# Slot outputs in two PSUM banks, a direct product for the first columns of S, a first gh in pieces, and dispatch maxima read from PSUM

## The chip, the core and the metric

The kernel runs on one NeuronCore of a Trainium2 chip. The metric is the device time of one execution in microseconds (us), median of several runs. A profile is one execution recorded by the hardware profiler; its span is a little shorter than that execution's device time. The engines are named PE (TensorE matmul), PEld (TensorE weight load), DVE (VectorE), ACT (ScalarE), POOL (GpSimd) and SP (SyncE, which issues the DMAs).

## The reference

Three stages follow each other; all data is fp32.

```python
# 1. attention: 8 batches, 8 heads, 576 queries of 64; keys and values are means over groups of 8
k_p = k.reshape(B, H, 72, 8, D).mean(axis=3);  v_p = the same of v
x = softmax(q @ k_p.T / 8) @ v_p               # x: 4608 tokens x 512
# 2. soft mixture of 8 experts with 4 slots each (32 slots)
logits = x @ phi
d = exp(logits - logits.max(0)); d /= d.sum(0)  # dispatch: over tokens
slot_input = d.T @ x                            # 32 x 512
slot_out[e] = relu(slot_input[e] @ w1[e]) @ w2[e]   # 512 -> 1024 -> 512
c = exp(logits - logits.max(1)); c /= c.sum(1)  # combine: over slots
x = c @ slot_out
# 3. feed-forward, 512 -> 2048 -> 512
g = s * relu(x @ w_in) ** 2 + b
out = g @ w_out
```

## The kernel before, in words

**Attention and dispatch.** A loop runs over 36 token tiles of 128 in a software pipeline of stages A to F; an order written out by hand (`LOOP`, `FIRST`, `PLAN1`, `PLAN2`) says in which order an iteration issues them, and each engine executes what it is given strictly in that order. Stage A transposes q (L362 on PE, copied by ACT at L364), B makes the scores (PE L392), their row maxima (DVE L399) and the difference (DVE L401), C the exponential (ACT L409), its sum (DVE L410) and the product P (POOL L430), D transposes P (PE L443, ACT L449), E and F make logits. `p` advances the pooling of k and v for the next pair of batches (DVE and POOL, L260 to L265; ACT L282). `r` advances every running `dispatch` by one piece, up to its next `yield`. A `dispatch` (one for each batch, eight in all) finds the 32 maxima of its batch's logits: a matmul at L558 spreads them over all partitions into a PSUM bank, DVE copies them to `m_all` (L559), one `r` later DVE subtracts them from the logits into `dd` (L562), one `r` later ACT takes the exponential (L564), and later ones sum `dd` (L569) and multiply it with P (PE L586). Matmul outputs of this stage take turns in a pool of four PSUM banks (`bank()`).

**Experts.** 32 weight tiles of 1 MB are loaded and used in the order of `EORD`; matmuls of the first layer are at L969, those of the second at L977. At L977 four matmuls with 32 output rows each (four quarters of the partitions) take 512 columns, in the bank `so_ps`, summed over all experts. An fp32 matmul shows as two records in the profile. While this runs, `step_convs` advances the conversion of the first columns of w_in and w_out (`narrow`, DVE, ACT, POOL).

**Hand-over.** After the last second-layer matmul two matmuls without use (`busy`, L1004) run on PE, `so_ps` is copied by ACT (L1008), four matmuls with a selection matrix sum the four quarters and transpose (L1011), ACT copies the result into `sot` (L1014). `S` is `slot_out @ w_in` in the layout that the third stage needs. For the first two blocks of 128 columns of S, `s_a` multiplies `sot` with a block of w_in in four quarters (PE L862), ACT copies (L868), `s_b` sums the quarters (PE L879), ACT rounds to fp32r (L884) and DVE forms the rest in the lower half (L885). The order of this stage is the string `OPS`; `o` in it advances the conversion of w_out (`conv_wo`: rounding to `wh` by ACT at L898, rest `wl` by POOL at L900, column sum `wsum` by POOL at L904 and L906).

**Third stage.** 24 blocks of 768 tokens are cut by `GROUPS` into 96 steps; in a step `st_h` makes h (two matmuls of 384 columns, L1050), ACT takes Relu and Square and rounds to `gh` (L1059, L1060, L1067), DVE forms `gl = r - gh` (L1079), and `st_o` adds 18 matmuls of 512 columns (six token tiles, three products gh wh, gh wl, gl wh; L1106). For step 0 `st_h` and `st_g` share the work in two halves between ACT (L1054, L1056, L1076) and DVE (L1055, L1057, L1077), and the h of step 1 is made by `OPS` too. h of step i+2 is made inside step i.

Of the kernel before, what the change touches and what calls it, by code (L numbers as in the profile page):

```python
# [18 lines left out]
OPS = "o0 a0 o0 a1 b0 b1 h0 g0 o1 h1 o1 g1"  # L19
# [5 lines left out]
BUSY = (2, 0)  # L25
# [34 lines left out]
def kernel(  # L60
# [481 lines left out]
    def dispatch(b_):  # L542
# [314 lines left out]
    def s_a(fs, ps):  # L857

        for i, f in enumerate(fs):
            t = t_wi.pop(f)  # L860
            for kc in range(4):
                nc.tensor.matmul(  # L862
                    out=ps[32 * kc:32 * kc + 32, 128 * i:128 * i + 128], lhsT=sot[:, kc, :], rhs=t[:, kc, :], start=True, stop=True
                )
        n, f = 128 * len(fs), fs[0]
        if f < 2:
            sps_t[f] = sps_f[:, 128 * f:128 * f + n]
            nc.scalar.copy(out=sps_t[f], in_=ps[:, 0:n])  # L868
            return
# [5 lines left out]
    def s_b(fs, ps):  # L875

        n, f = 128 * len(fs), fs[0]
        if f < 2:
            nc.tensor.matmul(out=ps[:, 0:n], lhsT=selrep.rearrange("p r s -> p (r s)"), rhs=sps_t.pop(f), start=True, stop=True)  # L879
        else:  # L880
            for i, x in enumerate(sps_t.pop(f)):
                nc.tensor.matmul(out=ps[:, 0:n], lhsT=selr, rhs=x, start=(i == 0), stop=(i == 1))
        S = Sw.rearrange("p f x -> p (f x)")[:, 128 * f:128 * f + n]
        nc.scalar.copy(out=S, in_=ps[:, 0:n])  # L884
        nc.vector.tensor_tensor(out=S[64:128], in0=ps[64:128, 0:n], in1=S[64:128].bitcast(F32), op=ALU.subtract)  # L885

    def conv_wo(f):
# [10 lines left out]
        nc.scalar.copy(out=wh, in_=t)  # L898
# [38 lines left out]
    so_ps = ps_1.tile([128, 512], F32, tag="so", name="so_ps")  # L937
# [22 lines left out]
    for n_, key in enumerate(EORD):  # L960
# [14 lines left out]
        else:  # L975
            for c in range(4):
                nc.tensor.matmul(  # L977
                    out=so_ps[32 * c:32 * c + 32, :],
                    lhsT=h1z[:, 4 * hf + c, 36 * ge + 16 - 4 * e:36 * ge + 48 - 4 * e],
                    rhs=w[:, c, :],  # L980
                    start=(e == 0 and hf == 0), stop=(e == E - 1 and hf == 1),
                )
# [264 lines left out]
```

## Time and profile before

| | us |
|---|---|
| median of 3 runs | 693.62 (692.23 to 693.72) |
| the profiled execution, device time | 692.57 |
| its span | 690.8 |
| PE busy | 649.7 (94% of the span) |
| attention and dispatch | 0 to 203 |
| experts | 203 to 245 |
| hand-over, last L977 matmul to first L1106 matmul | 245.2 to 251.6 |
| third stage | 251.6 to 690 |

Times in the text are from the start of the span. The profiled execution's device time is 1.8 us above its span and 1.05 us below the median of the runs. A busy share is an average over stages with different limits, so the stages are read one by one.

### The profile page before, as it was taken

How to read it: one execution, taken by the hardware profiler on the slowest of the kernel's cores; microseconds unless marked ns; L12 is line 12 of the kernel's file. 1: busy time of each engine (PE TensorE's matmuls, PEld its weight loads, DVE VectorE, ACT ScalarE, POOL GpSimd, SP SyncE). 2: the span in 40 equal slices, each digit the busy share in tenths (PEclk: the TensorE clock that was granted, in tenths of full speed). 3: DMA queues.
4: the chain of work that ended last, by engine and by line, in shares of the span. 5: the costliest groups of instructions: out<-in, count | busy, mean ns of one | idle time of the engine just before them, and what ended most of it. 6: DMA issues, size and time to landing. Idle time of an engine off the chain costs nothing.

```text
span 690.8 us, 11197 instructions
## 1 busy us (share of the span) xinstructions
PE 649.7 (94%) x4307; PEld 520.0 (75%) x4307; DVE 475.8 (69%) x748; ACT 399.9 (58%) x659; POOL 287.1 (42%) x220
## 2 busy tenths in 40 slices
PE   7877989799989889999999999999999999999996
PEld 6665777678653358888888888888888888888885
DVE  6879778767663947887677778887556764566443
ACT  3565667566421267886666666666666666555551
POOL 3766466522100443563223434443232241899200
PEclk9998999999679899999999999999999999999999
DMA  8999486607599992011110110301100000222222
GB/s 287 399 340 288 154 245 245 218 29 258 185 362 374 366 277 82 1 61 62 61 62 1 61 62 1 121 14 49 61 1 1 0 1 0 93 93 92 92 92 91
DMA packets 42085, 91.23 MB, mean 132 GB/s; under 512 B 7216, under 2 KB 15408, under 8 KB 42032
## 3 DMA queue, kind: packets, MB, share of 16 engines
q1 hardware_dynamic: 42032, 90.52, 38.4%
q8 instruction: 34, 0.56, 0.3%
q14 instruction: 19, 0.16, 0.1%
HBM read 78.71 MB, written 9.44 MB: 128 GB/s over the span
## 4 chain that ended last, share of the span: by engine, by line
PE 78%; DVE 11%; DMA 4%; ACT 3%; SPq 1%; issue 1%; POOL 0%; DVEq 0%; ACTq 0%
PE o L1106 57%; PE h L1050 5%; PE sc L392 3%; DMA x<-in_moe_w_dram 2%; PE l L969 2%; DVE S L401 2%; DVE mx L399 2%; DVE sm L410 2%; PE w L443 1%; DMA ring<-in_q_dram 1%; PE w L609 1%; ACT S L409 1%; PE w L362 1%; PE w L586 1%; PE w L466 1%
## 5 line engine op out<-in xcount | busy, mean ns | idle before, releaser
L1106 PE MATMUL o<-whi,gh 128*128 128x512 f32 x576 | 225.2, 391 | 1.2 <-ACT gh L1076 1.2
L1106 PE MATMUL o<-wlo,gh 128*128 128x512 f32 x576 | 224.9, 390 | 0.0
L1106 PE MATMUL o<-whi,gl 128*128 128x512 f32 x576 | 209.8, 391 | 0.0
L1079 DVE TENSOR_TENSOR gl<-r,gh 128x768 fp32r<-128x768 f32 (+1 forms) x97 | 104.8, 1081 | 116.4 <-ACT gh L1067 116.1
L1059 ACT ACTIVATE r<-h 128x768 f32<-128x768 f32 x95 | 77.5, 816 | 142.2 <-PE h L1050 140.3
L1106 PEld LDWEIGHTS o<-whi,gl 128*128 128x128 f32 x576 | 108.2, 188 | 22.8
L1106 PEld LDWEIGHTS o<-whi,gh 128*128 128x128 f32 x576 | 108.1, 188 | 21.5 <-ACT gh L1076 1.5
L1106 PEld LDWEIGHTS o<-wlo,gh 128*128 128x128 f32 x576 | 108.2, 188 | 18.9
L842 POOL TENSOR_TENSOR fr<-fr,xp 128x512 f32<-128x512 f32 x28 | 45.2, 1613 | 173.9 <-ACT fr L841 156.7
L1119 DVE SCALAR_TENSOR_TENSOR part<-o,sb_t,part 128x512 f32<-128x512 f32 x144 | 96.9, 742 | 3.2 <-PE o L1106 3.1
L1060 ACT ACTIVATE r<-r 128x768 f32<-128x768 f32 x95 | 80.5, 848 | 3.0
L1067 ACT CAST gh<-r 128x768 fp32r<-128x768 f32 x95 | 79.4, 835 | 2.6
L430 POOL TENSOR_TENSOR P<-S,rs 128x576 f32<-128x576 f32 x32 | 37.3, 1166 | 74.1 <-DVE rs L413 39.1
L1216 POOL TENSOR_TENSOR part<-part,wsum 128x512 f32<-128x512 f32 x36 | 53.3, 1518 | 15.1 <-ACT wsum L1210 15.1
L1050 PE MATMUL h<-cT,S 128*128 128x384 f32 x192 | 49.3, 338 | 0.5 <-DVE S L885 0.5
L1050 PEld LDWEIGHTS h<-cT,S 128*128 128x128 f32 x192 | 36.0, 188 | 8.7 <-DVE S L885 0.7
L410 DVE TENSOR_REDUCE sm<-S 128x8 f32<-128x584 f32 x36 | 27.3, 758 | 20.5 <-ACT S L409 20.4
L392 PE MATMUL sc<-kb,qT 128*128 128x144 f32 x256 | 40.5, 305 | 0.2 <-ACT qT L364 0.2
L399 DVE TENSOR_REDUCE mx<-sc 128x8 f32<-128x576 f32 x36 | 26.4, 733 | 15.6 <-PE sc L392 13.1
L392 PEld LDWEIGHTS sc<-kb,qT 128*128 128x128 f32 x256 | 36.4, 206 | 0.7 <-ACT qT L364 0.5
L409 ACT ACTIVATE S<-S 128x576 f32<-128x576 f32 x36 | 24.6, 682 | 19.4 <-DVE S L401 19.1
L364 ACT COPY qT<-w 128x512 f32<-128x512 f32 x36 | 20.9, 584 | 21.6 <-PE w L362 20.9
(236 smaller groups left out, 884.6 us busy)
## 6 DMA issues: line engine op xcount, KB each, us to landing
x<-in_moe_w_dram SPq DMA_DIRECT2D x15, 1024.0 KB, 9.7
ring<-in_moe_w_dram SPq DMA_DIRECT2D x12, 1024.0 KB, 6.4
raw<-in_moe_w_in_dram SPq DMA_DIRECT2D x8, 1024.0 KB, 5.7
raw<-in_moe_w_out_dram SPq DMA_DIRECT2D x8, 1024.0 KB, 4.8
out_dram<-part SPq DMA_DIRECT2D x32, 256.0 KB, 2.7
ring<-in_q_dram SPq DMA_DIRECT2D x7, 1024.0 KB, 10.8
ring<-in_v_dram SPq DMA_DIRECT2D x9, 768.0 KB, 10.5
ring<-in_k_dram SPq DMA_DIRECT2D x7, 768.0 KB, 8.1
```

Source lines behind the costliest of these rows:

```text
L392: nc.tensor.matmul(out=sc[:, i // 2, 2 * KP * (i % 2):2 * KP * (i % 2) + 2 * KP], lhsT=qT[:, i, :], rhs=kb[:, H * bb + 4 * (j % 2) + i, :] ...
L399: nc.vector.tensor_reduce(out=mx, in_=scv, axis=AX.X, op=ALU.max)
L410: nc.vector.tensor_reduce(out=sm, in_=S, axis=AX.X, op=ALU.add)
L842: nc.gpsimd.tensor_tensor(out=fr, in0=fr, in1=xp, op=ALU.mult)
L1050: nc.tensor.matmul(out=h[x][:, 0:384] if i == 0 else h[:, x, 0:384], lhsT=Sw[:, f, :], rhs=cT(c, 384), start=True, stop=True)
L1059: nc.scalar.activation(out=r, in_=h[:, :, 0:384], func=ACTF.Relu)
L1060: nc.scalar.activation(out=r, in_=r, func=ACTF.Square)
L1067: nc.scalar.copy(out=gh_t[i], in_=r)
L1079: nc.vector.tensor_tensor(out=gl[:, x], in0=r[:, x], in1=gh[:, x].bitcast(F32), op=ALU.subtract)
L1106: nc.tensor.matmul(out=o_t[tt], lhsT=l[:, x, 128 * c:128 * c + 128], rhs=r, start=(fi == 0 and n == 0), stop=(fi == GROUPS[g] - 1 and n == 1),
L1119: nc.vector.scalar_tensor_tensor(out=p, in0=o_t[tt], scalar=sb_t[:, 0:1], in1=p, op0=ALU.mult, op1=ALU.add)
L1216: nc.gpsimd.tensor_tensor(out=p, in0=p, in1=wsum, op=ALU.add)
```

## The change

- **Dispatch.** `dd` is formed from the PSUM bank itself, right behind the matmul; the exponential comes one `r` earlier than before, and the copy to `m_all` moves behind it into that later `r`. No instruction is added or taken away.
- **Slot outputs.** Each second-layer matmul of 512 columns becomes two of 256, for the two halves of the columns, into two banks. ACT copies the first half, DVE the second. The transposes go into two banks too and are copied by ACT and DVE, each value written four times side by side (`sot` has 128 columns now).
- **busy.** The two matmuls without use have 128 columns of the identity and no longer read `cT` (the transposed combine weights, which DMAs write).
- **First S.** `s_direct` makes the first two blocks of S with four full matmuls each, summed in PSUM; the copy at L868 and the sum at L879 go.
- **OPS and step 0.** The first `gh` is made in three pieces: 128 columns by DVE alone, 256 and 384 with Relu by ACT and the product by DVE, written straight into `gh`; ACT squares `r` afterwards, for `gl`. The h of step 1 moves from `OPS` into the matmuls of step 0, behind the sixth; step 0 issues all its gh matmuls ahead of the gl ones. For step 1 too DVE makes gh as a product. The rounding of the second w_out block (f = 1) goes to DVE.
- **Scratch.** One buffer of the six of `th_all` is taken from `L_all` instead of the pool.

```diff
-OPS = "o0 a0 o0 a1 b0 b1 h0 g0 o1 h1 o1 g1"
+OPS = "o0 a0 a1 o1 o0 o1 c0 u0 c1 h0 w1 u1 g0"
...
-        nc.vector.tensor_copy(out=m_all[:, b_, :], in_=ps[:, 0:32])
-        yield
-        dd = ap2.tile([128, 5, 32], F32, tag="dd", name="dd")
-        nc.vector.tensor_tensor(out=dd, in0=Lb, in1=m_all[:, b_, :].unsqueeze(1).to_broadcast([128, 5, 32]), op=ALU.subtract)
-        yield
-        nc.scalar.activation(out=dd, in_=dd, func=ACTF.Exp)
+        dd = ap2.tile([128, 5, 32], F32, tag="dd", name="dd")
+        nc.vector.tensor_tensor(out=dd, in0=Lb, in1=ps[:, 0:32].unsqueeze(1).to_broadcast([128, 5, 32]), op=ALU.subtract)
+        yield
+        nc.scalar.activation(out=dd, in_=dd, func=ACTF.Exp)
+        nc.vector.tensor_copy(out=m_all[:, b_, :], in_=ps[:, 0:32])
+        yield
         yield
...
+    def s_direct(f, ps):
+        t = t_wi.pop(f)
+        for kc in range(4):
+            nc.tensor.matmul(
+                out=ps, lhsT=sot[:, kc].rearrange("p r s -> p (r s)"), rhs=t[:, kc, :], start=(kc == 0), stop=(kc == 3)
+            )
...
-        nc.scalar.copy(out=wh, in_=t)
+        (nc.vector.tensor_copy if f == 1 else nc.scalar.copy)(out=wh, in_=t)
...
-            for c in range(4):
-                nc.tensor.matmul(
-                    out=so_ps[32 * c:32 * c + 32, :],
+            for x in range(2):
+                for c in range(4):
+                    nc.tensor.matmul(
+                        out=so_ps[x][32 * c:32 * c + 32, 0:256],
...
+                        rhs=w[:, c, 256 * x:256 * x + 256],
...
-            nc.tensor.matmul(out=ps, lhsT=cT(0, 128), rhs=cT(0, 512), start=True, stop=True)
-    busy(l1[0][0], BUSY[0])
+            nc.tensor.matmul(out=ps, lhsT=ident, rhs=ident, start=True, stop=True)
+    busy(l1[1][0][:, 0:128], BUSY)
...
-    nc.scalar.copy(out=so, in_=so_ps)
...
-    nc.scalar.copy(out=sot, in_=sot_ps)
+    copies = nc.scalar.copy, nc.vector.tensor_copy
+    for x in range(2):
+        copies[x](out=so[:, 256 * x:256 * x + 256], in_=so_ps[x][:, 0:256])
+    for x in range(2):
+        for kc in range(2):
+            c0 = 256 * x + 128 * kc
+            nc.tensor.matmul(out=sot_ps[x][:, kc, :], lhsT=so[:, c0:c0 + 128], rhs=sel4, start=True, stop=True)
+        copies[x](out=sot[:, 2 * x:2 * x + 2], in_=sot_ps[x].unsqueeze(2).to_broadcast([128, 2, 4, 32]))
...
+    def square(i, r, pieces):
+        gh = gh_t[i] = fp2.tile([128, 2, 384], F32R, tag="gh", name="gh")
+        for x, c in pieces:
+            nc.vector.tensor_tensor(out=gh[:, x, c], in0=r[:, x, c], in1=r[:, x, c], op=ALU.mult)
+        for x in (0, 1) if i == 0 else (slice(0, 2),):
+            nc.scalar.activation(out=r[:, x], in_=r[:, x], func=ACTF.Square)
...
         if i == 0:
-            nc.scalar.activation(out=r[:, 0], in_=h[0][:, 0:384], func=ACTF.Relu)
-            nc.vector.tensor_scalar(out=r[:, 1], in0=h[1][:, 0:384], scalar1=0.0, scalar2=None, op0=ALU.max)
-            nc.scalar.activation(out=r[:, 0], in_=r[:, 0], func=ACTF.Square)
-            nc.vector.tensor_tensor(out=r[:, 1], in0=r[:, 1], in1=r[:, 1], op=ALU.mult)
+            c1, c2 = slice(0, 128), slice(128, 384)
+            nc.vector.tensor_scalar(out=r[:, 0, c1], in0=h[0][:, c1], scalar1=0.0, scalar2=None, op0=ALU.max)
+            nc.scalar.activation(out=r[:, 0, c2], in_=h[0][:, c2], func=ACTF.Relu)
+            nc.scalar.activation(out=r[:, 1], in_=h[1][:, 0:384], func=ACTF.Relu)
+            square(i, r, ((0, c1), (0, c2), (1, slice(0, 384))))
...
     def st_g(i, r):
+        if i == 1:
+            square(i, r, ((slice(0, 2), slice(0, 384)),))
...
+        if i == 0 and 1 not in ns:
+            todo_ = [(tt, n) for tt in range(NG) for n in ns] if tts == (0,) else []
+        elif i == 0:
+            todo_ = [(tt, 1) for tt in tts]
+        for j, (tt, n) in enumerate(todo_):
+            if i == 0 and j == 6:
+                r_[1] = st_h(1)
...
     for op in OPS.split():
-        elif op[0] == "a":
-            s_a((n,), scratch(2 * n))
-        elif op[0] == "b":
-            s_b((n,), scratch(2 * n + 1))
+        if op[0] == "a":
+            sd[n] = scratch(3 * n)
+            s_direct(n, sd[n])
+        elif op[0] == "c":
+            nc.scalar.copy(out=Sw[:, n, :], in_=sd[n])
+        elif op[0] == "u":
+            nc.vector.tensor_tensor(out=Sw[64:128, n, :], in0=sd[n][64:128], in1=Sw[64:128, n, :].bitcast(F32), op=ALU.subtract)
```

## Rows read from the trace of the kernel before

**Rows 1.** The page's chain that ended last, shares by line.
```profile
PE o L1106 57%; PE h L1050 5%; PE sc L392 3%; DMA x<-in_moe_w_dram 2%; PE l L969 2%; DVE S L401 2%; DVE mx L399 2%; DVE sm L410 2%; PE w L443 1%; DMA ring<-in_q_dram 1%; PE w L609 1%; ACT S L409 1%; PE w L362 1%; PE w L586 1%; PE w L466 1%
```

**Rows 2.** Busy time by stage: stretch, length, engines, granted clock, DMA share, GB/s.
```profile
65.00:200.00 135.00, 122.23 (x1477) 98.22 (x1475) 98.79 (x203) 81.08 (x207) 55.84 (x50) 0.95 0.59 205
...
245.00:252.00 7.00, 4.49 (x40) 3.20 (x37) 2.31 (x6) 4.33 (x12) 1.26 (x1) 1.00 0.86 194
252.00:690.00 438.00, 433.44 (x2038) 361.54 (x2036) 296.18 (x408) 275.21 (x356) 179.95 (x125) 1.00 0.16 56
```

**Rows 3.** Timeline of the hand-over: start, us, engine, line, operation, [idle before it].
```profile
242.42 1.03 PE L977 MATMUL so_ps<-ring,ring 128*32 128x512 f32 x8
...
243.28 1.89 PE L977 MATMUL so_ps<-x,ring 128*32 128x512 f32 x16
...
245.30 0.59 ACT L1008 COPY si_all<-so_ps 128x512 f32<-128x512 f32 x1 [6.83 <-PE so_ps L977]
...
245.99 1.03 PE L1011 MATMUL sot_ps<-sel,si_all 128*128 128x32 f32 x8
...
247.05 0.27 ACT L1014 COPY sot<-sot_ps 128x128 f32<-128x128 f32 x1 [1.17 <-PE sot_ps L1011]
247.27 0.62 ACT L898 CAST whi<-ring 128x512 fp32r<-128x512 f32 x1
...
247.97 1.26 POOL L900 TENSOR_TENSOR wlo<-ring,whi 128x512 fp32r<-128x512 f32 x1 [3.51 <-DMA cT<-ring]
...
249.13 0.52 DVE L885 TENSOR_TENSOR S<-o,S 64x128 fp32r<-64x128 f32 x2 [7.45 <-DMA cT<-ring]
...
249.48 0.97 PE L1050 MATMUL h<-cT,S 128*128 128x384 f32 x4 [0.46 <-DVE S L885]
...
249.96 0.49 ACT L1054 ACTIVATE r<-h 128x384 f32<-128x384 f32 x1 [0.64 <-DMA cT<-L]
250.13 0.56 DVE L1055 TENSOR_SCALAR r<-h 128x384 f32<-128x384 f32 x1 [0.48 <-PE h L1050]
...
251.03 0.51 ACT L1076 CAST gh<-r 128x384 fp32r<-128x384 f32 x1
...
251.60 0.50 PE L1106 MATMUL o<-whi,gh 128*128 128x512 f32 x1 [1.15 <-ACT gh L1076]
...
254.08 0.61 POOL L904 COPY wsum<-ring 128x512 f32<-128x512 f32 x1
...
254.46 0.51 PE L1050 MATMUL h<-cT,S 128*128 128x384 f32 x2
```

**Rows 4.** The tiles dd, m_all and S: count, ns min/median/max, first and last start.
```profile
L562 DVE TENSOR_TENSOR dd<-L,m_all x8: 317/679/1860, 69.5 to 195.4; 128x160 f32<-128x160 f32 x8
...
L559 DVE COPY m_all<-w x8: 178/180/192, 66.0 to 195.2; 128x32 f32<-128x32 f32 x8
...
L401 DVE TENSOR_TENSOR S<-sc,mx x36: 757/758/760, 15.0 to 181.5; 128x576 f32<-128x576 f32 x36
```

**Rows 5.** Timeline around the first two dispatches, by engine.
```profile
69.61 0.99 ACT L282 ACTIVATE kb<-w 64x384 f32<-64x384 f32 x2
71.14 0.34 ACT L564 ACTIVATE dd<-dd 128x160 f32<-128x160 f32 x1 [0.54 <-DVE dd L562]
...
72.45 0.49 PE L275 MATMUL w<-ident,kp 128*64 128x128 f32 x3 [1.05 <-ACT LT L478]
...
90.80 1.80 POOL L260 TENSOR_TENSOR ring<-ring 128x768 f32<-128x768 f32 x1
90.92 1.86 DVE L562 TENSOR_TENSOR dd<-L,m_all 128x160 f32<-128x160 f32 x1
...
92.82 0.34 ACT L564 ACTIVATE dd<-dd 128x160 f32<-128x160 f32 x1 [1.87 <-DVE dd L562]
93.06 0.67 ACT L409 ACTIVATE S<-S 128x576 f32<-128x576 f32 x1
93.27 0.69 PE L586 MATMUL w<-P,dd 128*32 128x288 f32 x8 [0.75 <-ACT dd L564]
```

More of the change, by code (lines that the diff above doesn't have):

```diff
@@ L862, in s_a @@
                 nc.tensor.matmul(
-                    out=ps[32 * kc:32 * kc + 32, 128 * i:128 * i + 128], lhsT=sot[:, kc, :], rhs=t[:, kc, :], start=True, stop=True
+                    out=ps[32 * kc:32 * kc + 32, 128 * i:128 * i + 128], lhsT=sot[:, kc, 0, :], rhs=t[:, kc, :], start=True, stop=True
                 )
         n, f = 128 * len(fs), fs[0]
[L866 to L869, printed above, removed]
         hi, lo = sps[:, 0:n], sps_l[:, 0:n]
@@ L877, in s_b @@
         n, f = 128 * len(fs), fs[0]
[L878 to L882, printed above, removed]
+        for i, x in enumerate(sps_t.pop(f)):
+            nc.tensor.matmul(out=ps[:, 0:n], lhsT=selr, rhs=x, start=(i == 0), stop=(i == 1))
         S = Sw.rearrange("p f x -> p (f x)")[:, 128 * f:128 * f + n]
@@ L1003, in busy @@
         for _ in range(n):
-            nc.tensor.matmul(out=ps, lhsT=cT(0, 128), rhs=cT(0, 512), start=True, stop=True)
-    busy(l1[0][0], BUSY[0])
+            nc.tensor.matmul(out=ps, lhsT=ident, rhs=ident, start=True, stop=True)
+    busy(l1[1][0][:, 0:128], BUSY)
     so = si_all.rearrange("p b c s -> p (b c s)")[:, 0:DM]
-    nc.scalar.copy(out=so, in_=so_ps)
-    sot_ps = ps_1.tile([128, 4, 32], F32, tag="hps", name="sot_ps")
-    for kc in range(4):
-        nc.tensor.matmul(out=sot_ps[:, kc, :], lhsT=so[:, 128 * kc:128 * kc + 128], rhs=sel4, start=True, stop=True)
-    sot = cv.tile([128, 4, 32], F32, name="sot")
-    busy(l1[0][0], BUSY[1])
-    nc.scalar.copy(out=sot, in_=sot_ps)
+    sot_ps = [p.tile([128, 2, 32], F32, tag=t_, name="sot_ps") for p, t_ in ((ps_1, "hps"), (ps_x, "sx"))]
+    sot = cv.tile([128, 4, 4, 32], F32, name="sot")
+    copies = nc.scalar.copy, nc.vector.tensor_copy
[6 more added lines that the diff above has]
+        copies[x](out=sot[:, 2 * x:2 * x + 2], in_=sot_ps[x].unsqueeze(2).to_broadcast([128, 2, 4, 32]))
     while convs:
@@ L1069, in st_g @@
     def st_g(i, r):
-        if i == 0:
-            gh = fp2.tile([128, 2, 384], F32R, tag="gh", name="gh")
-        else:
-            gh = gh_t.pop(i)
+        if i == 1:
+            square(i, r, ((slice(0, 2), slice(0, 384)),))
+        gh = gh_t.pop(i)
         gl = fp2.tile([128, 2, 384], F32R, tag="gl", name="gl")
-        if i == 0:
-            nc.scalar.copy(out=gh[:, 0], in_=r[:, 0])
-            nc.vector.tensor_copy(out=gh[:, 1], in_=r[:, 1])
         for x in (slice(0, 1), slice(1, 2)) if i == 0 else (slice(0, 2),):
@@ L1143 @@
         elif op[0] == "w":
-            busy(ps_o.tile([128, 512], F32, tag="o3", name="o3"), n)
+            busy(scratch(1), n)
         else:
@@ L1153 @@
     scr_pool.append(ctx.enter_context(tc.tile_pool(name="scr", bufs=1)))
[L1154 removed]
+    th_all.extend(scr_pool[0].tile([128, 512], F32, name=f"th{i}") for i in range(2))
     th_all.extend(hs[:, 512 * i:512 * i + 512] for i in range(2))
[L1156 removed]
+    th_all.extend(L_all.rearrange("p j r s -> p (j r s)")[:, 512 * i:512 * i + 512] for i in range(2))
     i0 = 0
```

28 lines of the change are left out of this document (12 added, 16 removed).

## The prediction

> **What bounds the kernel now.** I read the chain that ended last first [rows 1]: 57% of the span is L1106 and 5% L1050, both of the third stage. Then busy time by stage [rows 2]: from 252 to 690 PE is busy 433.4 of 438 us at a granted clock of 1.00 (2.4 GHz), so that stage ends when PE has done a fixed list of matmuls, and the change takes none of them away. What can move is the time at which it starts. Two stretches ahead of it are touched. In the hand-over, 245 to 252, PE is busy 4.49 of 7 us: the timeline [rows 3] is to be read as one chain that passes from PE to ACT, PE, ACT, PE, ACT, DVE, PE, ACT and PE, from the last L977 matmul (243.28 + 1.89 = 245.17) to the first L1106 at 251.60, 6.43 us. In the attention loop, 65 to 200, no engine is full (PE 122.2 of 135 us, DVE 98.8, ACT 81.1), so in-order waits set its pace. There I looked for the dispatch instructions alone: the subtraction L562 takes 0.317 us at best, 0.679 in the median and 1.86 at worst [rows 4], and the timeline around the first two [rows 5] says why and who waits.
>
> **Dispatch.** The second L562 starts at 90.92, just behind the POOL addition of 90.80 to 92.60, and ends at 92.78: it stood until POOL had finished. ACT has the exponential of dd next in its order, sat idle 1.87 us for it, and so the exponential of the scores (L409) came at 93.06 although its input, L401's output, was there at about 91.0. The new subtraction has one input in SBUF and one in PSUM. L401 is of that kind, ran 36 times through the same loop and took 757 to 760 ns every time [rows 4], with POOL busy 55.8 of 135 us [rows 2]: it is never held. So I price the new dd at 0.32, and it also comes ahead of L401 rather than behind it, where the copy stood (+0.14 on DVE there, 0.18 in its old place, both less than what they replace). The exponential, one `r` earlier, waits for nothing.
>
> What is released: at the first dispatch ACT had finished L282 at 70.60 and idled until the exponential at 71.14; L409 follows that by 0.24 (as 93.06 follows 92.82), so it can come 0.78 us earlier; PE had been idle 1.05 us behind that same ACT order at 72.45, so PE can use it all. At the second, ACT is released by 2.0 us (93.06 to 91.05), but PE shows idle of only 0.75 us for that exponential; I count 0.75. For the six others I count nothing: these two are the longest waits, and half of all L562 are at or under 0.68. Sum **1.5 us**. Bounds: 2.8 if both delays pass in full, 0 if PE's other work fills the space. For a loss there is a reason only in rival D.
>
> Loads do not hold this gain back by themselves: they are issued as slots come free, and slots come free by the work that moves forward.
>
> **Hand-over, step by step** [rows 3], in times of the profiled execution.
>
> - *L977 in halves.* A weight tile takes 0.86 us (242.42 to 243.28). The columns stay the same in number; twice the instructions of half the width I cost at nothing (covered by the streaming of the columns; if a quarter-matmul cost 10 ns more, eight tiles would give 0.3 us). The first half is ready 0.43 earlier.
> - *Copies.* 256 columns lie between ACT's 0.27 for 128 (L1014) and 0.49 for 384 (L1054): 0.38, from 244.87. On DVE, 0.56 for 384 (L1055) and 0.18 for 32 (L559) give 1.08 ns a column: 0.42, from 245.30 to 245.72; before, ACT ended at 245.89.
> - *busy and transposes.* Four records of 128 columns, by L1011 (eight in 1.03) about 0.5, stand ahead of the transposes, from 245.0. These start at 245.5 instead of 245.95, and the copies are there when needed: 0.45 earlier, sum ready at 246.57.
> - *sot.* Its second half is a DVE copy of 0.42 where ACT took 0.27: 247.07 against 247.32, 0.25 earlier.
> - *First S.* The direct product takes eight records (1.03) but half of them run on the first half of `sot`; the other four end at 247.75. ACT's rounding 0.27 and DVE's 0.29 (two in 0.52, overlapped) give 248.4; the second block's eight records leave PE by 248.5. So h of step 0 starts at 248.5 instead of 249.48: 0.98 earlier. If matmuls wait for both halves, 0.45 of it is lost.
> - *First gh.* h is read at 248.98. Three ACT passes (249.96 to 251.54) become two DVE instructions of 128 columns: 0.28 (L1055's slope) and 0.28 (L562's 0.317 less 32 columns). Without other work in the way L1106 starts at 249.65, 1.95 earlier.
> - *What is in the way.* The product r times r has two inputs in SBUF, like the old dd. POOL now makes both wl (1.26 each, L900) back to back behind wh, from 247.2 to 249.85; before, the second came after the first L1106. By the 0.18 us that dd ended behind POOL, the product ends at 250.05, and L1106 starts at **250.1: 1.5 earlier**.
> - *What moves into PE's list.* The two matmuls of h of step 1, 0.35, ran in idle time and now stand between L1106 matmuls: minus 0.35. They wait for DVE's second block of S, which is queued behind two more products (0.42, 0.56), each of which can find POOL busy (L904, 0.61): ready at 251.8, wanted at 250.1 + 6 x 0.238 = 251.5: minus 0.35 with the signal.
> - *Step 1.* Its gh is one DVE product and its Square follows on ACT, then gl on DVE: about 0.1 late.
>
> Sum 1.5 - 0.35 - 0.35 - 0.1 = **0.7 us**. Bounds: 1.6 with nothing held (1.95 - 0.35), 0 if the matmuls wait for the whole sot and one more instruction of DVE is held. What is later than step 1 I cost at nothing: PE's list covers it, as before. The scratch buffer too: its users come in the third stage, where DVE and ACT are busy 296 and 275 of 438 us and PE alone is full [rows 2].
>
> The Trainium skill, "SBUF — State Buffer", section "SBUF: two separate sides", says that VectorE and GpSimd share one pair of ports as an exclusive lock, held for the whole instruction, by a VectorE instruction with two SBUF inputs against a GpSimd one that reads SBUF. The trace agrees: 1.86 us against 0.317. It speaks for the dispatch part and against the gh part, where three products are new on DVE; by it the sum stays 2.2, and 1.5 if the second product is held in full as well.
>
> **Sum.** 692.57 - 1.5 - 0.7 = 690.4 for the profiled execution, which lies 1.05 below the median of the runs: 691.4 against 693.62. A change of less than 0.2% (1.4 us) can hardly be told from none.
>
> **Rivals.**
> - *A, as summed*: 691.4. Chance 0.50.
> - *B, the dispatch gain is lost on the way*: PE is busy 90% of the loop, and what ACT gains is eaten by its next wait. Only the hand-over counts: 692.9. Against it stand the named idle times of PE. Chance 0.20.
> - *C, POOL takes the hand-over's gain*: the second product is held behind another long POOL instruction as well (1.26 by L900's row, 0.6 more than L904), so the second block of S, h of step 1 and everything behind it come 0.7 later; only the dispatch counts: 692.1. For it: POOL is full from 247.2 on. Against it: only the first three pieces must come in time. Chance 0.17. This is the lock of the Trainium skill's page at its hardest.
> - *D, the bank held longer stops PE: slower.* The bank of L558 is now read until the copy to `m_all`, which stands on DVE behind L399 and L401 of the next iteration. Three tiles take a bank in between (one of F or E, two of D); the fourth is A's, and its transposes would stop PE until the copy: maxima, difference and copy behind the scores, by L401 and L559 about 0.76 + 0.76 + 0.18 = 1.7 us, in six dispatches 10.2, less the idle time of PE (12.8 us in 135; an iteration takes 4.76 us, by the first and last start of 36 L401, so 0.45 of it each): 7.5 us, so 693.62 + 7.5 - 0.7 = 700.4. It decides from 0.82 us of stop per dispatch, where 6 x (0.82 - 0.45) has used up 2.2 us. Against it: for the fourth dispatch two tiles of `p` come in as well, and D itself would wait for a copy that stands behind D's followers, which would never end; so the pool must give out the bank that came free first, and A gets F's or E's. Chance 0.08.
> - *E, nothing moves*: both gains fall into waits for something else, 693.6. Chance 0.05.
>
> **Numbers.** The likeliest is A, 691.4. Low end: both parts at their upper bounds, 693.62 - 2.8 - 1.6 = 689.2. High end: B with the hand-over at 0.3, 693.3. Outside are D, E and what noise adds. A's own range is 689.2 to 692.3. Faster by over 0.2%: A and C, 0.67. Same: B and E, 0.25. Slower: D, 0.08.
>
> **What would show it.** L562 eight times near 0.32 to 0.4 us; ACT without an idle 1.87 us ahead of it, and the first expert matmul (L969) about 1.5 us earlier; the transposes of the slot outputs about 0.45, h of step 0 about 1, the first L1106 about 1.5 us earlier relative to the last L977. The product at the first gh long (near 0.8 us) if POOL holds it, 0.28 if not. L362 idle behind DVE's copy would mean D; an L969 that does not move, B; a first L1106 early but gaps between the first twelve, C. The prediction is wrong if the loop's order turns the released time into another wait, or if the granted clock falls from 1.00 in the new, shorter hand-over [rows 2].

## The result, and the profile after

The kernel before takes 693.67 us (median of four runs beside the changed one), the changed kernel 686.58 (685.83 to 687.86): a ratio of 0.9898, 95% interval 0.9875 to 0.9922. That is 7.1 us, where the forecast was 2.2 and the range went down to 689.2. The direction was right and the size was not. Another chip gave 686.38 against 693.92 (0.9907, 0.9880 to 0.9934).

The profiled execution took 685.83 us with a span of 684.0. Its page shows the same bound as [rows 1], the two shares of the third stage unchanged, and windows by stage that answer to [rows 2] (stretch, length, busy time and instructions of PE, PEld, DVE, ACT, POOL, granted clock, DMA share, GB/s):

```profile
65.00:194.00 129.00, 118.17 (x1476) 94.51 (x1475) 94.39 (x203) 81.69 (x207) 55.86 (x50) 0.99 0.59 209
239.06:243.91 4.85, 4.16 (x33) 3.85 (x33) 2.43 (x7) 2.13 (x7) 2.82 (x3) 1.00 0.95 221
243.91:678.22 434.31, 434.21 (x2039) 361.81 (x2040) 297.02 (x410) 275.32 (x357) 178.53 (x124) 1.00 0.16 54
```

The 1476 matmul records of the loop need 118.17 us of busy TensorE where 1477 needed 122.23, and the granted clock of the stretch is 0.99 instead of 0.95. No edit touches those matmuls; in the main they are the same work at a higher clock. That is the first sign of what the forecast left out.

The dispatch's tiles (count, ns min/median/max, first and last start), for [rows 4]:

```profile
L560 DVE TENSOR_TENSOR dd<-L,w x8: 308/309/322, 66.0 to 189.2; 128x160 f32<-128x160 f32 x8
...
L563 DVE COPY m_all<-w x8: 180/180/183, 69.5 to 189.5; 128x32 f32<-128x32 f32 x8
```

All eight differences take 0.31 us, as L401's kind led to expect. Around the second dispatch (timeline; for [rows 5]):

```profile
85.78 0.31 DVE L560 TENSOR_TENSOR dd<-L,w 128x160 f32<-128x160 f32 x1
...
87.38 0.34 ACT L562 ACTIVATE dd<-dd 128x160 f32<-128x160 f32 x1
...
90.31 0.68 ACT L409 ACTIVATE S<-S 128x576 f32<-128x576 f32 x1
...
91.92 0.69 PE L586 MATMUL w<-P,dd 128*32 128x288 f32 x8
```

The exponential of dd runs 2.9 us ahead of L409 in ACT's order, and L409 no longer stands behind it. L409 comes at 90.31 instead of 93.06, L586 at 91.92 instead of 93.27.

The hand-over (timeline; for [rows 3]):

```profile
238.75 0.37 ACT L1016 COPY si_all<-so_ps 128x256 f32<-128x256 f32 x1 [6.94 <-PE so_ps L981]
...
238.99 0.71 PE L1008 MATMUL l<-ident 128*128 128x128 f32 x4
...
239.19 0.42 DVE L1016 COPY si_all<-so_ps 128x256 f32<-128x256 f32 x1 [4.17 <-ACT si_all L1016]
...
239.54 0.98 PE L1020 MATMUL sot_ps<-sel,si_all 128*128 128x32 f32 x8
...
240.55 0.42 DVE L1021 COPY sot<-sot_ps 128x256 f32<-128x256 f32 x1 [0.94 <-PE sot_ps L1020]
...
242.48 0.62 PE L1064 MATMUL h<-cT,S 128*128 128x384 f32 x2
...
243.29 1.46 DVE L1050 TENSOR_TENSOR gh<-r 128x128 fp32r<-128x128 f32 x3
...
243.91 0.50 PE L1124 MATMUL o<-whi,gh 128*128 128x512 f32 x1 [0.59 <-DVE gh L1050]
...
245.41 0.51 PE L1064 MATMUL h<-cT,S 128*128 128x384 f32 x2
```

From the last so_ps matmul (239.06) to the first o matmul it is 4.85 us instead of 6.43, and the third stage behind it takes 434.31 instead of 433.39: 0.66 gained in all, against 0.7 worked out.

Between the two lies the surprise. From the start of tile 33's L401 (tiles count from 0; below "tile 33's scores") to the first expert matmul the windows are, for before and for the changed kernel:

```profile
171.01:203.21 32.20, 28.13 (x283) 21.55 (x282) 20.44 (x53) 11.10 (x32) 5.02 (x5) 0.76 0.71 261
```

```profile
168.75:196.97 28.22, 23.23 (x282) 18.06 (x282) 20.32 (x53) 10.87 (x31) 5.01 (x5) 0.94 0.76 284
```

The same 282 or 283 matmul records take 28.13 us of TensorE in one and 23.23 in the other, at a clock of 0.76 and 0.94; DVE's busy time is 20.4 and 20.3. Before, the granted clock is 0.50 (1.2 GHz) from 177.44 to 191.09 and again from 201.33; after, from 180.69 to 184.10 alone. One place, in the order of the list, before and after:

```profile
178.29 2.27 PE L392 MATMUL sc<-kb,qT 128*128 128x144 f32 x8
180.35 1.81 PE L619 MATMUL w<-a,vps 72*128 72x64 f32 x8
```

```profile
175.19 1.23 PE L392 MATMUL sc<-kb,qT 128*128 128x144 f32 x8
176.25 1.00 PE L619 MATMUL w<-a,vps 72*128 72x64 f32 x8
```

So the span's 6.75 us are: 2.26 up to tile 33's scores, 3.98 from there to the first expert matmul, -0.13 in the experts, 0.66 behind them, and nothing at the end (5.80 and 5.82).

### The profile page after: what moved, and what is told of

It reads as the page before. It is cut to its first block, busy times and chain, and to the rows that moved or that the text cites. A ratio compares the mean times of both kernels' runs of the same rounds, so it can differ in the third digit from the quotient of the medians.

```text
span 684.0 us, 11450 instructions
## 1 busy us (share of the span) xinstructions
PE 645.8 (94%) x4435; PEld 520.9 (76%) x4435; DVE 473.4 (69%) x753; ACT 398.8 (58%) x656; POOL 287.3 (42%) x220
## 4 chain that ended last, share of the span: by engine, by line
PE 80%; DVE 9%; DMA 5%; ACT 3%; issue 1%; SPq 1%; DVEq 0%; ACTq 0%
PE o L1124 57%; PE h L1064 5%; PE sc L392 3%; DMA x<-in_moe_w_dram 2%; PE w L443 2%; DVE S L401 2%; PE l L970 2%; DVE mx L399 1%; DVE sm L410 1%; PE w L362 1%; PE w L609 1%; DMA ring<-in_q_dram 1%; PE w L586 1%; ACT S L409 1%; PE w L466 1%
## 5 line engine op out<-in xcount | busy, mean ns | idle before, releaser
L392 PE MATMUL sc<-kb,qT 128*128 128x144 f32 x256 | 39.1, 298 | 0.2 <-ACT qT L364 0.2
L409 ACT ACTIVATE S<-S 128x576 f32<-128x576 f32 x36 | 24.7, 685 | 18.6 <-DVE S L401 17.4
```

Source lines behind the costliest of these rows:

```text
L392: nc.tensor.matmul(out=sc[:, i // 2, 2 * KP * (i % 2):2 * KP * (i % 2) + 2 * KP], lhsT=qT[:, i, :], rhs=kb[:, H * bb + 4 * (j % 2) + i, :] ...
```

## The experiments

Times are medians beside the kernel before on the same chip, with the ratio and its 95% interval; "clock" is the mean granted clock of an execution. In the end 104 timed runs of the kernel before lay between 689.35 and 699.24 us at clocks of 0.961 to 0.983, and a straight line through them falls by 0.34 us for each 0.001 of clock. "Tail" is from tile 33's scores to the first expert matmul; "behind the experts" is from the end of the last so_ps matmul to the end of the last o matmul that reads whi and gh (two more o matmuls, 0.46 us, come behind it).

**The two parts alone.** Dispatch alone is the diff's hunk at L556 put into the kernel before; hand-over alone is the changed kernel with the old lines there.

> The kernel before with the new dispatch alone: the difference formed from PSUM, ahead of the copy, its exponential one r earlier; all of the hand-over as before. Theory 1 (the dispatch gives some 2.5 us by its waits and as much again because the TensorE work behind it, at the end of the attention loop, no longer runs at the 1.2 GHz level from 177 to 191 us): 6 to 6.5 us faster than before, mean granted clock 0.977 to 0.981 instead of 0.969, first L969 about 6 us earlier. Theory 2 (the clock at the loop's end differs for another reason, as the hand-over or chance): 1.5 to 2.7 us faster, clock 0.969.

> The changed kernel with the old dispatch: the two banks, the direct S and the gh in pieces alone. Theory 1: 0.7 us faster than before, clock 0.969, the first expert matmul where it was (203.2), the first o matmul (of whi and gh) about 1.6 us nearer to the last so_ps matmul. Theory 2 (the hand-over is worth more than was summed, 3 to 4 us of the 7.1): 3 to 5 us faster, with the loop up to 200 us unchanged.

Dispatch alone: 689.86 against 693.51 (0.9939, 0.9918 to 0.9959), clock 0.969 to 0.980. Hand-over alone: 692.31 (0.998, 0.996 to 1.000), clock 0.970 to 0.980. The first lies between the two theories, and together they give less than the whole. In the profiles the dispatch alone reached tile 33's scores at 168.97 (before: 171.01), its tail took 29.37, and 440.05 lay behind the experts. The hand-over alone took 171.83, 30.51 and 439.07. Single executions of one kernel differ by more than these differences, so the places are compared over several profiles below.

**Order or operand.** The dispatch makes two edits at once.

```diff
 e3 (order alone)
         nc.vector.tensor_copy(out=m_all[:, b_, :], in_=ps[:, 0:32])
-        yield
         dd = ...
         nc.vector.tensor_tensor(out=dd, in0=Lb, in1=m_all[:, b_, :]..., op=ALU.subtract)
         yield
         nc.scalar.activation(out=dd, in_=dd, func=ACTF.Exp)
         yield
+        yield
 e4 (operand alone)
-        nc.vector.tensor_tensor(out=dd, in0=Lb, in1=m_all[:, b_, :]..., op=ALU.subtract)
+        nc.vector.tensor_tensor(out=dd, in0=Lb, in1=ps[:, 0:32]..., op=ALU.subtract)
```

> The kernel before with the dispatch's difference and exponential one r earlier, right behind the copy to m_all, but still from m_all in SBUF. Theory L (what counts is that the difference from two SBUF inputs is held by POOL): several of the eight differences still take over 0.6 us, the second named wait of ACT (1.87 us) or a like one stays, 0 to 1.5 us faster, and the 1.2 GHz stretch from 177 us stays as long as it was. Theory O (what counts is the exponential's earlier place in ACT's order): 4 to 6.5 us faster.

> The kernel before with the difference formed from PSUM, but at its old r, behind the copy of the r before, and the exponential in its old place. Theory L: all eight differences take 0.31 to 0.35 us, and the gain is nearly that of the whole dispatch part (direct 1.5 to 2.5 us; with the shorter 1.2 GHz stretch 4 to 6.5). Theory O: 0 to 1.5 us faster.

Order alone: 690.22 (0.9948, 0.9926 to 0.9971). Operand alone: 691.59 (0.9963, 0.9943 to 0.9984). The two differences of dd, e3's first:

```profile
L561 DVE TENSOR_TENSOR dd<-L,m_all x8: 324/326/1476, 65.1 to 189.9; 128x160 f32<-128x160 f32 x8
```

```profile
L562 DVE TENSOR_TENSOR dd<-L,w x8: 310/311/313, 68.3 to 190.2; 128x160 f32<-128x160 f32 x8
```

With the order alone a difference still stands behind POOL for 1.48 us, and it no longer matters, because ACT has other work in the meantime:

```profile
106.65 1.82 POOL L260 TENSOR_TENSOR raw<-raw 128x768 f32<-128x768 f32 x1
...
107.17 1.48 DVE L561 TENSOR_TENSOR dd<-L,m_all 128x160 f32<-128x160 f32 x1
...
107.31 0.68 ACT L409 ACTIVATE S<-S 128x576 f32<-128x576 f32 x1
...
107.90 0.57 ACT L449 COPY PT<-w 128x512 f32<-128x512 f32 x1
...
108.36 0.26 ACT L450 COPY PT<-w 64x128 f32<-64x128 f32 x1
...
108.68 0.34 ACT L563 ACTIVATE dd<-dd 128x160 f32<-128x160 f32 x1
```

Both rivals L and O fall as exclusive ones: at the second dispatch (tile 12's to tile 17's scores) before takes 25.43 us, order alone 24.23, operand alone 24.17, both 24.03. Each edit by itself removes most of that wait, and the second adds little. The two differ at one other place: from tile 33's to tile 34's scores the order alone takes 3.58 us, as the change does (3.59), and the operand alone 4.04, as before. In e3 the hold of 1.48 us costs nothing where it falls: from tile 17's to tile 33's scores e3 takes 70.03 us, the change 70.02 to 70.05. The Trainium skill ("SBUF — State Buffer", "SBUF: two separate sides") has VectorE with two SBUF inputs and a GpSimd instruction that reads SBUF lock each other out. The trace agrees: up to 1.476 us with two SBUF inputs, 0.313 at most with one in PSUM.

**Whether idle time of TensorE sets the clock.** Unread matmuls of the identity, put where TensorE stood idle: nine in the kernel before (e5), 28 in the changed one (e6).

```diff
 e5
+    37: "F C E w3 D r B p r A",
...
             z_spread(nc.scalar.copy)
+            if b_ == B - 3:
+                warm(6)
 e6 (and warm(5) in the same place)
-... X0 D2 6 X1 ... M3 6 7 M4 7"
+... X0 D2 W11 6 X1 ... M3 6 7 M4 W6 7 W6"
```

> The kernel before, with nothing of the change, and nine matmuls of the identity by itself whose result nobody reads, put where TensorE stood idle just before the long stretch at 1.2 GHz: three ahead of L443 (idle 174.89 to 175.35) and six ahead of L609 (176.04 to 176.83). Theory 1 (the clock fell because TensorE stood idle there, and the change's larger half is that stretch): the granted clock from 177 to 191 us is 1.00 for most of it, the first L969 comes 3 to 4.5 us earlier and the whole is 2.5 to 4 us faster, with the loop up to 172 us as it was. Theory 2 (the clock's fall has another cause, or the matmuls behind it do not set the pace there): 0 to 0.5 us faster, or slower by the nine matmuls' 1.2 us at most.

> The changed kernel with unread matmuls of the identity in the four places where TensorE stands idle in the attention's last part: five ahead of L609 (173.32 to 174.13), eleven ahead of L553 (178.03 to 179.63), six ahead of L619 (193.99 to 194.92) and six ahead of the first L970 (196.03 to 196.97). Theory 1: the two stretches at 1.2 GHz that are left there (180.69 to 184.1 and 197.76 to 201.17) go; each made up to 3.4 us of matmuls take twice their time, so up to 1.7 us each; the second is not worth that much because the last expert weights then come too late (TensorE already waits 0.46 us for one at 237.52): 0.7 to 2 us faster than the changed kernel. Theory 2 (idle time of TensorE ahead of a stretch does not set its clock): the clock stays 0.979 and the time is that of the changed kernel or later by up to 0.5 us.

e5: 693.03 against 694.50 (0.9989, 0.9967 to 1.0012), clock 0.969 to 0.980. In its profile the long stretch at 1.2 GHz from 177 us was gone (3.41 us from 187.70 in its place), but the fill waited 0.76 us for a PSUM bank, and the tail was 30.95. e6: 690.10 (0.9934, 0.9907 to 0.9960), clock 0.984 to 0.989, the highest so far, and slower than the changed kernel had been (686.58, on another chip). Filling the idle time raised the clock in both (e5's mean is 0.977, before's beside it 0.971). In e6 the fills cost more than the clock gives back; in e5 no gain is seen. Theory 1 came in neither. Two more tries put them into the waiting matmul's own bank (e8) and behind the last users of one (e12); of each one place of four:

```diff
 e8
         ps = bank()
+        fill(ps[:, 128:256], {6: 10}.get(b_, 0))
         nc.tensor.transpose(out=ps[0:32, 0:128], in_=md, identity=ident)
 e12
         nc.scalar.copy(out=PT[0:64, 4, r], in_=pb[0:64, 0:128])
+        fill(pb[:, 128:256], 5 if t == NT - 3 else 0)
```

> The changed kernel with the idle places of TensorE ahead of L609, L553, L619 and the first L970 filled again with unread matmuls of the identity (5, 10, 6 and 6), this time into unused columns of the very bank that the waiting matmuls write, so that they take no bank of their own. Theory 1: the stretches at 1.2 GHz behind them go as in the filled kernel before this one (mean clock 0.984 or more), without its delays (the first L970 within 0.3 us of the changed kernel's or earlier): 0.5 to 2 us faster than the changed kernel, held by the last expert weights. Theory 2 (the clock in the attention's end is worth nothing, because the weights' transfers set the end of the experts): same time as the changed kernel within 0.5 us though the clock is higher.

> The changed kernel with fewer unread matmuls in the idle places of the attention's last part, each behind the matmuls that use a bank, into columns of it that nobody reads, so that none waits for a bank: three behind L573 (ahead of L609), five behind L444 (ahead of L553), three behind L609 and three behind L619. In the filled kernel before, one took 0.25 us (two records), twice what was reckoned, so that eleven delayed the tail. Theory 1: no delay now, no 1.2 GHz from 180 to 201 us, clock 0.984 or more, the tail from tile 35's scores to the first L970 18.5 to 19.2 us instead of 19.65, 0.5 to 1 us faster than the changed kernel, no more since the last weights set the end of the experts. Theory 2 (matmuls put there delay others whatever their number): 19.7 us or more, and not faster.

e8: 688.86 (0.9936, 0.9910 to 0.9962) at a clock of 0.984 to 0.989, tail 31.78. e12: 694.62 (0.9979, 0.9949 to 1.0008), tail 37.44. Theory 2 of e12 holds. The rows of e8 and of e12 (timeline) say why:

```profile
180.23 2.47 PE L250 MATMUL w<-ident 128*128 128x128 f32 x20 [0.69 <-DVE si_all L636]
182.53 0.27 PE L558 MATMUL w<-ident,md 128*32 128x128 f32 x1
```

```profile
173.92 0.94 PE L250 MATMUL w<-ident 128*128 128x128 f32 x6 [1.52 <-ACT z_all L579]
```

A fill needs a bank that is free: in e8 it waited 0.69 us until DVE (L636), in e12 1.52 us until ACT (L579) had read the bank, and then stood in front of the real work; and one fill is two records, 0.25 us, twice what was reckoned. No version that beats the changed kernel came of it.

**Draw or rule.** Profiles of one kernel differ, so each was taken again.

> The changed kernel as it is, beside more runs of the kernel before. Seen so far: runs of one and the same kernel differ by some 7 us, and go with the mean granted clock of the execution (0.961 to 0.982 for before, some 0.33 us for each 0.001). Theory 1 (2.5 us of the change are work that no longer waits, 0.7 the hand-over, and the change makes stretches at 1.2 GHz rarer besides): mean clock 0.976 or more, 5 to 7 us faster than before. Theory 2 (the four runs with 0.979 to 0.981 were luck, and the clock's odds are the same before and after): mean clock 0.972, about 3.3 us faster (2.5 + 0.7).

> The kernel before, unchanged, for a second profile. Theory 1 (where the 1.2 GHz stretches lie is drawn anew in each execution): stretches at other points than 177.44 to 191.09 and 201.33 to 208.16, another sum of them, and the span follows that sum. Theory 2 (they belong to the program): the same stretches within 1 us.

> The kernel before, unchanged, a third profile. Theory 1 (the old dispatch leaves TensorE idle in the attention's last part, and the old hand-over ahead of the third stage, so that each often costs clock): from tile 33's scores to the first L969 30 to 32.5 us with 8 us or more at 1.2 GHz, and from the last so_ps matmul to the last o matmul 439.8 to 444 us. Theory 2 (both differences are draws of an execution, whatever the code): a tail of 28 to 29.5 us with 6.5 us or less at 1.2 GHz is as likely as any.

> The dispatch alone, a second profile of the same kernel. Theory 1: tail 28 to 29.8 us with 3 to 7 us at 1.2 GHz; hand-over and third stage 439.8 to 444 us, as with the kernel before. Theory 2: tail 30 to 32.5 us as likely as any.

> The changed kernel, a third profile. Theory 1: tail 28 to 29.8 us; from the last so_ps matmul to the last o matmul 439.1 to 439.2 us, no 1.2 GHz between 238 and 260 us. Theory 2: tail 30 us or more, or a stretch at 1.2 GHz behind the hand-over.

> The hand-over alone (old dispatch), a second profile. Theory 1: tail 30 to 32.5 us as with the kernel before, and from the last so_ps matmul to the last o matmul 439.1 us without a stretch at 1.2 GHz. Theory 2: a tail of 28 to 29.5 us, or a stretch at 1.2 GHz behind the hand-over.

The changed kernel again (e7): 686.38 against 693.92 (0.9907, 0.9880 to 0.9934), six runs at clocks of 0.978 to 0.982. With the first four and e15 (685.59, 0.979) all eleven lie there, while the 104 of before average 0.971 and eight of them reach 0.980. Theory 2 of e7 is out; the 7.5 us lie just above theory 1's 5 to 7. In e9 the stretches lie elsewhere than in before (from 183.41 instead of 177.44), as its theory 1 has it. The stages of ten profiles, in us, with the us at 1.2 GHz in brackets (worked out from the granted clock's stretches):

```
                    to S of 33   tail         experts  behind the experts
before              171.01       32.20 (15.5)  41.96   439.82 (0)
before, e9          171.81       30.58 (8.7)   41.93   442.61 (6.8)
before, e13         172.82       30.60 (8.9)   44.44   442.15 (6.8)
hand-over, e2       171.83       30.51 (8.6)   42.27   439.07 (0)
hand-over, e16      172.18       30.65 (9.1)   44.25   439.54 (0)
dispatch, e1        168.97       29.37 (6.3)   42.37   440.05 (0)
dispatch, e14       167.81       30.15 (8.5)   42.16   444.26 (10.2)
change              168.75       28.22 (3.4)   42.09   439.16 (0)
change, e7          169.05       28.32 (3.4)   41.33   439.18 (0)
change, e15         168.07       28.25 (3.4)   42.34   439.35 (0)
```

Two columns separate by the code, the first and the last. With the old dispatch the loop is 2 to 5 us longer. A part of that comes in every execution: from tile 5's to tile 12's scores the three profiles of before take 36.31 to 36.33 us and those of the change 35.58 to 35.61, from tile 12's to tile 17's 25.43 to 25.44 and 24.02 to 24.04, from tile 33's to tile 34's 4.04 and 3.58 to 3.60. The rest does not: in four profiles of eight with the old dispatch (e5, e9, e13, e16) a further stretch at 1.2 GHz lies at 136 us. From tile 17's to tile 33's scores these four take 71.64 to 71.76 us, the other four 70.08 to 70.19, so it costs 1.5 us. In e9 it stands behind this wait of TensorE:

```profile
134.34 0.52 PE L275 MATMUL w<-ident,vp 128*64 128x128 f32 x3 [2.08 <-POOL vp L265]
```

The first profile of before has the same wait (2.08 us at 135.07) and not the stretch. None of the twelve profiles with a cured dispatch has the stretch; the wait is 1.38 us in the change's first. The windows of 130 to 145 us, e9 and the change:

```profile
130.00:145.00 15.00, 12.92 (x157) 10.14 (x157) 8.89 (x16) 8.45 (x24) 4.99 (x5) 0.89 0.52 190
```

```profile
130.00:145.00 15.00, 13.43 (x203) 10.40 (x200) 9.31 (x19) 9.50 (x25) 5.28 (x6) 1.00 0.44 149
```

Behind the experts the old hand-over lies between 439.8 and 444.3 us and the new one between 439.1 and 439.5 (e12, whose last stretch at 1.2 GHz reaches 1.1 us into this part, 439.6). The first 15 us from the last so_ps matmul, e9's, then e16's:

```profile
244.33:259.33 15.00, 12.17 (x60) 9.63 (x61) 8.10 (x13) 9.13 (x17) 5.71 (x6) 0.77 0.96 296
```

```profile
247.07:262.07 15.00, 14.23 (x77) 11.81 (x76) 11.12 (x20) 9.90 (x19) 6.72 (x7) 1.00 0.93 284
```

The old hand-over leaves TensorE idle for some 2.5 of 6.4 us, and in three of these five profiles its third stage then starts at 1.2 GHz: 60 matmul records in 15 us instead of 77. The forecast's execution was one of the other two.

The tail is the column that the code does not settle. It goes with the place where the first stretch at 1.2 GHz behind tile 33's scores falls. With the whole new dispatch and no fill in the tail, that stretch starts 11.94, 12.15 and 12.01 us behind tile 33's scores in the change's three profiles, 12.81, 12.93 and 12.96 us in e1, e11 and e18, and 11.37 us in e14. (e11 and e18 follow below: e11 has the old hand-over, e18 is the change up to the end of the experts.) The windows of the tail in e1, e18 and e14:

```profile
168.97:198.34 29.37, 24.23 (x282) 18.44 (x282) 20.32 (x53) 10.86 (x31) 5.02 (x5) 0.89 0.75 284
```

```profile
168.49:197.87 29.38, 24.24 (x283) 18.38 (x282) 20.30 (x53) 10.86 (x31) 5.02 (x5) 0.89 0.76 285
```

```profile
167.81:197.96 30.15, 25.08 (x282) 18.84 (x282) 20.40 (x53) 10.88 (x31) 5.02 (x5) 0.86 0.76 273
```

The same place gives the same tail (28.2 to 28.3, three times 29.4), whatever the hand-over behind it, and the same code up to there gives three places. The old dispatch has as many: 6.43 and 6.55 us in before and e17 (tails of 32.20 and 32.13), 7.12 in e10 (30.17), 11.27 to 11.68 in e9, e13, e2 and e16 (30.51 to 30.65). At nearly the same place as e14's these last are 0.4 to 0.5 us longer, about the 0.45 that tile 33 to 34 shows in every execution. So most of the 3.98 us of the first two profiles' tails is where the stretches happened to fall. Theory 1 of e13 came, and of e15 and e16 but for 0.2 and 0.4 us behind the experts; for the tail of e14 (30.15, 8.5 us at 1.2 GHz) theory 2 did.

**What in the hand-over keeps the clock.** Six unread matmuls in the idle places of the old one, without (e10) and with (e11) the new dispatch:

```diff
-OPS = "o0 a0 o0 a1 b0 b1 h0 g0 o1 h1 o1 g1"
+OPS = "o0 a0 o0 a1 b0 b1 h0 w4 g0 o1 h1 o1 g1"
-BUSY = (2, 0)
+BUSY = (2, 2)
```

> The kernel before with six more unread matmuls of 512 columns in its hand-over, where TensorE stands idle: two behind the transposes (idle 247.02 to 247.46) and four behind h of step 0 (250.45 to 251.60). Nothing of the change. Theory 1 (in the slow executions of before the third stage starts at 1.2 GHz because TensorE is idle in the hand-over): no run with a clock below 0.968, 0.5 to 1.5 us faster in the mean. Theory 2: clock and time as before within 0.3 us.

> The kernel before with the new dispatch and the old hand-over, whose idle places of TensorE are filled with six unread matmuls (as in the filled kernel before: two behind the transposes, four behind h of step 0). So far the stretch from the last so_ps matmul to the last o matmul was 439.1 us in every profile with the new hand-over, and 439.8 to 444.0 with the old one, whose long ones show 6.8 to 10.2 us at 1.2 GHz at the third stage's start. Theory 1 (the new hand-over's larger worth is that TensorE is not idle long enough there to lose its clock): that stretch is 439.8 to 440.7 here, no 1.2 GHz between 240 and 260 us, mean clock about 0.978, and the whole 4.5 to 5.5 us faster than before, against 3.5 for the dispatch alone. Theory 2 (filling does nothing, only the shorter chain does): as the dispatch alone, 3.5 us faster at a clock of 0.975.

e10: 692.47 against 693.92 (0.9988, 0.9966 to 1.0009), clock 0.967 to 0.982, 440.64 us behind the experts with nothing at 1.2 GHz. e11: 688.54 against 694.79 (0.9909, 0.9876 to 0.9941), clock 0.976 to 0.982, 440.03. Theory 1's profile came in both. Its time came in e11, whose interval still overlaps the dispatch's alone, and not in e10, where two runs are at 0.967 and theory 2's 0.3 us isn't excluded. Since e1 without the fill also had no 1.2 GHz there, the fill's worth stays inconclusive.

In ten profiles with the old hand-over busy's matmuls waited 0.25 to 1.43 us for cT, which a DMA brings; the change lets them read the identity, 128 columns instead of 512. That edit alone (e17), and it alone undone (e18):

```diff
 e17
-            nc.tensor.matmul(out=ps, lhsT=cT(0, 128), rhs=cT(0, 512), start=True, stop=True)
+            nc.tensor.matmul(out=ps, lhsT=ident, rhs=ident, start=True, stop=True)
 e18
-    busy(l1[1][0][:, 0:128], BUSY)
+    for _ in range(BUSY):
+        nc.tensor.matmul(out=l1[1][0], lhsT=cT(0, 128), rhs=cT(0, 512), start=True, stop=True)
```

> The kernel before with one thing of the change: the two unread matmuls of busy (L1004), which stand ahead of the slot outputs' transposes in TensorE's order, read the identity instead of cT, which a DMA brings. In ten profiles with the old hand-over TensorE stood idle 0.25 to 1.43 us ahead of L1004 (0.25 in the profile that the forecast was made from); the four with 1.2 us or more all show 1.2 GHz at the third stage's start. Theory 1 (this wait, not in the forecast, is what makes the old hand-over's cost vary): no idle over 0.3 us there, from the last so_ps matmul to the last o matmul 439.3 to 440.2 us, the slowest runs of before (clock 0.966 and less) gone, 1 to 2 us faster in the mean. Theory 2 (the transposes or h wait for something else then, and the clock falls all the same): 440.5 to 444 us there, within 0.5 us of before.

> The changed kernel with that one thing undone: the two matmuls of busy read cT again (512 columns, as in the kernel before). Theory 1: TensorE idle up to 1.4 us ahead of them, the stretch from the last so_ps matmul to the last o matmul 439.3 to 441 us instead of 439.1, 0.3 to 1.5 us slower than the changed kernel (686.4), clock 0.974 to 0.98. Theory 2 (h of step 0 needs cT at nearly the same time, so that the wait is only moved): 439.1 to 439.3 us, time as the changed kernel.

e17: 693.71 against 694.62 (0.9995, 0.9966 to 1.0024). The wait is gone, and the third stage still starts at 1.2 GHz (441.91 us behind the experts):

```profile
245.26 0.71 PE L1004 MATMUL l<-ident 128*128 128x128 f32 x4
```

```profile
245.33:260.33 15.00, 13.06 (x65) 10.23 (x66) 8.76 (x14) 9.76 (x19) 5.69 (x6) 0.77 0.96 298
```

Theory 1 is wrong. e18: 688.23 (0.9907, 0.9873 to 0.9942), clock 0.975 to 0.985; its profile has 439.48 behind the experts and no 1.2 GHz there, though busy waits 0.30 for cT. What this execution (689.52 us) loses lies in its tail (29.38) and in the experts (44.61, TensorE waiting 1.18 and 0.85 us for weights), ahead of the edit, and the ratio of its runs is that of the change again. Of nine profiles with the old hand-over and no fill in it, seven have a stretch at 1.2 GHz in the first 15 us behind the last so_ps matmul (all but before and e1); of eight with the new one none has (e12 apart: the change's three, e2, e6, e8, e16 and e18). By these counts it is the new hand-over as a whole that keeps the clock, and not busy's operand. That its shorter chain does it, with less idle time of TensorE, is the likely reading: a long wait for cT never came with the new hand-over, and none of its other parts was run alone.

## Why the prediction was wrong in size

The step that failed is the sum itself, 1.5 + 0.7. It added up waits alone and took every matmul at the length that one execution showed, so it put the granted clock at nothing: the prediction names it only as something that might fall, in the new hand-over. What the runs showed is that the waits give 3.3 us and that the old code besides loses clock, in some executions, at two places where the new one does not. Step by step:

*Dispatch, the difference itself*: right. 0.31 us eight times, never held, and no stop of L362: rival D is out, as are E and B.

*Dispatch, what is released*: mis-sized. The first dispatch gives 0.72 where 0.78 was counted (tile 12's scores, 75.39 to 74.67). For the second, where ACT's 2.0 was cut down to TensorE's visible idle of 0.75, it gives 1.41 (25.43 to 24.02). "For the six others I count nothing" is wrong as well: at the sixth, the exponential goes out of L409's way (tile 33's to 34's scores 4.04 to 3.59), 0.45. Before, ACT idled 0.90 us for it there although that difference (0.32 us) was not held:

```profile
172.03 0.34 ACT L564 ACTIVATE dd<-dd 128x160 f32<-128x160 f32 x1 [0.90 <-DVE dd L562]
```

The place in the order counted there, not the hold. Together the three give some 2.6 of waits, inside the bounds of 0 to 2.8, instead of 1.5.

*Hand-over*: right, step by step (the transposes' old start is 245.99 in the rows, not 245.95, which changes nothing). The transposes end 0.39 earlier relative to the last so_ps matmul (0.45 forecast), h of step 0 0.89 (0.98), the first o matmul 1.58 (1.5), what moves into TensorE's list 0.92 back (0.8). The three products took 1.46 us; by the rows priced, 0.28 + 0.42 + 0.56 = 1.26, so POOL held them little, and C is out.

*What the sum had no term for*: the granted clock. The profiled execution had 1.2 GHz for 15.5 us of its tail and 2.4 GHz behind the experts; others of the same kernel have it elsewhere. By waits alone the forecast's terms measure 2.6 + 0.66, 3.3 us, and the three profiles of each kernel repeat the 2.6. All 104 runs of before average 694.1 at a clock of 0.971, the change's eleven 686.6 at 0.980: 7.5 us. By the straight line 2.8 of these go with the mean clock, and 1.4 more than the waits are left. The mean prices a stretch badly: the 3.41 us at 136 lower it by 0.0025, 0.8 us by the line, and cost 1.5.

By place, as an estimate from the profiles: the stretch at 136 us costs 1.5 in half of them, 0.75; behind the experts the nine profiles with the old, unfilled hand-over average 442.3 and the eight with the new one 439.2, of which 0.66 is waits, so 2.4; the tails of seven profiles of each dispatch (without e3, e4 and the filled ones) average 31.0 and 29.0, of which 0.45 is waits, so 1.5. With the 3.3 of waits that makes some 8, where the runs have 7.5. The first two of the three terms go with the code; the third rests on where the stretches fell, and these profiles are too few to say how often they fall where.

The sum's own profile hid this. Between that execution and the change's first, 3.98 of 6.75 us lay in the tail, where before had its longest stretch at 1.2 GHz and the change its shortest. That those two met is luck.

Open stays what sets the place of the stretches in an execution, and so how much of the tail's difference the change can claim.

## What to carry to other kernels

Two cures for one in-order wait, an earlier place and an operand that isn't held, were worth hardly more than one of them here. Look at the granted clock in and behind the stage of an edit before pricing it: where TensorE falls to 1.2 GHz behind idle time, an edit that shortens the idle time can be worth more than the wait itself, and one profile can't tell which stretches the next execution has. Take several profiles, and compare stretches of the program that begin and end at the same instruction. Filling idle time with unread matmuls raised the clock in three of four tries in the loop and paid in none: in each a fill waited 0.7 to 1.5 us for a PSUM bank and then stood ahead of the real work.

## What the hardware showed that was not expected

One kernel's runs on one chip spread over 7 us (689.35 to 696.64, 29 runs), and the spread goes with the granted clock. The first stretch at 1.2 GHz starts at 22.98 to 24.18 us in the three profiles each of before and of the change, and the next two shift with it. These six don't show what sets it, since tile 1's scores shift by as much (19.16 to 20.11 us). Others do: e2 and the change's second profile run the same program up to there, with tile 1's scores at 20.11 us in both, and the stretch starts at 23.08 and at 24.18; e3, e4, e12 and e14 have none before 45 us. The Trainium skill ("TensorE: Matmul & The Clock Gate", "What's actually happening") says that the clock gate's window runs freely and doesn't reset when the kernel starts. These starts agree.

A higher clock gains little where TensorE waits for data: e6 and e8 had the highest clocks of all (0.986 in the mean) and longer experts' stages (44.20 and 43.65 us), with TensorE idle for 2.57 and 1.65 us ahead of a late weight; the changed kernel's first profile already waits 0.46 us for one, at a DMA share of 1.02.
